# S4D convolution beside a gated linear unit on one core: 64-point sums of the spectra split by parity into 32-point sums

## The chip, the cores and the metric

One Trainium2 chip, one NeuronCore. The metric is the device time of one execution in microseconds (us), a median over runs; lower is better. Engines: PE (TensorE: matmuls; PEld is its weight load), DVE (VectorE), ACT (ScalarE), POOL (GpSimd), SP (SyncE, which issues most DMA transfers). Each engine takes its instructions in a fixed order and waits on semaphores. PSUM is PE's output memory, in banks of 2 KB a partition; SBUF is the working memory.

## What is computed

`u` is 2048 x 448 (L x D), N is 256, F is 1792. Cut to what matters:

```python
xn = layernorm(u)
dt = exp(log_dt); A = -exp(log_A_real) + 1j*A_imag; C = (C_real + 1j*C_imag)*dt[:, None]
P  = exp((A*dt[:, None])[:, :, None] * pos)               # D x N x L
K  = 2*einsum("dn,dnl->dl", C, P).real                    # the convolution's kernel
y  = irfft(rfft(xn.T, 2*L) * rfft(K, 2*L), 2*L)[:, :L].T  # causal convolution
out = u + y + xn*D_skip + (sigmoid(xn @ w_gate) * (xn @ w_up)) @ w_down
```

All matmul operands are 32-bit; the GLU's are split into a high and a low part (`xh`, `xl`, `wh`, `wl`, `dh`, `dl`, `hh`, `hl`), three products each.

## The kernel before

The Fourier transform of length 4096 is done as matrix products in stages. A first stage (of x in `x_spec` and `pair_first`, of K in `first_stage`) writes partial spectra to DRAM (`x1_d`, `sk_d`): for each of 33 residues k of the frequency a column of 64 blocks b, real and imaginary. The stage that the change is about, `spectra` (L850), then takes 17 steps. A step covers half of the channels (H = 224) and four residues k (one step holds the residue 32 of both halves). In a step:

- `loads` (L870) brings `sx` and `skl` (the partial spectra of x and of K) and the table `tb` of cosines and sines; loads stand three steps ahead (NLD = 3, L51).
- `there` (L896) does the 64-point sums over b: for each pair of residues and each of K and x it issues four matmuls of a 128x64 tile (L912; a matmul of 32-bit operands is two records in the trace, so 32 records a step), into PSUM tiles `sp` of one bank each, from a pool of four. ACT copies K's sum to SBUF (`kc`, L920). DVE forms the complex product of both: two products (L923, L924), reading x's sum in PSUM, a subtract and an add (L925, L926), into `yy`.
- `back` (L930) does the inverse sums of the product that the step before left in `yy`: eight matmuls of 64x128 tiles (L939), into tiles `pv` of the same four-bank pool. ACT copies them to `vt` (L948), and four transfers store them to `v_d` in DRAM (L959). `turned` (L961) loads `vp` from there in another order (L965).
- `last` (L967) does the last inverse stage once half of the channels is complete: 64 matmuls a half of 64x32 tiles (L976), added to the residual and GLU sums by DVE (L984).

In a step of the loop (L1006 to L1037) `back` of the step before comes first, then `there`, loads, at times `last`.

K itself comes from the kernel generator, `kgen` (L459): 56 chunks (NCK) of exponentials on ACT, DVE and POOL (L517, L526, L547, L550, L604 to L606) and matmuls `ko` (L620). After every four chunks `first_stage` issues 32 matmuls (64 records) of 64x64 tiles (`kp`, `kq`, L565), four tiles side by side.

The GLU is a second generator, `glu` (L733): `gate` (L699) issues 11 matmuls (L712) for the gate and 11 for the up product of 512 rows by 128 columns of F, then `th` on ACT (L720), `hf` on DVE (L723), `hh` on ACT (L728), `hl` on DVE (L730). The down matmuls `po` (L826) follow for a group of F tiles and are added to `acc` by DVE (L831). Some weights are split on the spot, not read back from DRAM: POOL loads them (`wraw`, L646 and L648), casts and subtracts (`wh` L774, `wl` L775), loads `rdw` (L654), casts and subtracts (`dh` L800, `dl` L801).

What sets the order: the main loop (L1138 to L1152) runs the two generators by pace. Each `yield` counts work units; the generator whose share of its `total` is smaller goes next. `total` of the convolution holds a term of 14 units ahead of the chunks, 56 x WK (5.5), and 17 x WS (4.5) for the spectra. `tc.issue_after` ties the matmuls of both to this order on PE; the order on DVE, ACT and POOL is fixed by a scheduler when the program is built. Buffers come from tile pools; a tile waits until all readers of the one that had its place before are done.

Of the kernel before, what the change touches and what calls it, by code (L numbers as in the profile page):

```python
# [15 lines left out]
ALU = mybir.AluOpType  # L16
# [14 lines left out]
WS = 4.5  # L31
HOLE = 6
WS = 4.5
# [24 lines left out]
def _tables():  # L58
# [16 lines left out]
    k2 = np.arange(64)[None, :]  # L75
    tab = np.zeros((NK1, 128, 128))
    bk = np.zeros((2, 2, 64, 2, 128))
    for q in range(NK1):
        al = 2 * np.pi * ((b * (q + 64 * k2)) % 4096) / 4096.0
        c, s = np.cos(al), np.sin(al)  # L80
        tab[q] = np.block([[c, -s], [s, c]])
        if q in (0, 32):


            for h in range(2):

                split = lambda t: t.reshape(64, 2, 32).transpose(0, 2, 1)
                both = lambda r, i: np.stack([split(r), split(i)], 3).reshape(64, 128)
                bk[q // 32, h, :, 0] = both(c.T, s.T)
                bk[q // 32, h, :, 1] = both(-s.T, c.T)  # L90

    tab[0, 64:] = 0.0
    t32 = np.concatenate([tab[32][:, None], bk[1].reshape(128, 2, 128)], 1)
    tab = tab[:32].reshape(8, 4, 128, 128).transpose(0, 2, 1, 3)

    wf = np.zeros((2, 2, 4, 8, 32, NA))
    for k in range(32):
# [5 lines left out]
        wf[:, 0, k % 4, k // 4] = re.reshape(2, 32, NA)  # L103
        wf[:, 1, k % 4, k // 4] = im.reshape(2, 32, NA)

# [7 lines left out]
    for row, tb_ in ((DC, 0), (64 + 2 * DC, 1)):  # L115
# [5 lines left out]
        "c_tab": f(tab, (8, 128, 4, 128)),  # L121
        "c_t32": f(t32, (128, 3, 128)),
        "c_bk": f(bk[0], (128, 2, 128)),
# [7 lines left out]
def s4d_glu_kernel(ctx, tc, io):  # L131
# [12 lines left out]
    x1_d = dram.tile([64, NB, D], F32, name="x1_d")  # L144
# [133 lines left out]
    def row(b, g):  # L278
        return 32 * (b // 4 % 2) + 8 * g + 4 * (b // 8) + b % 4
# [7 lines left out]
    def x_spec(xn, b0):  # L287

        for p in range(2):
# [7 lines left out]
            for i in range(2):  # L297
                r = row(b0 + i, 2 * p)
                nc.sync.dma_start(x1_d[:, r : r + 9 : 8], x1[64 * i : 64 * i + 64])
# [159 lines left out]
    def kgen(pk):  # L459
# [3 lines left out]
            ("sk", [128, 32, 32], F32), ("ks", [128, 8, 64], F32),  # L463
# [89 lines left out]
        def first_stage(bank):  # L553
# [7 lines left out]
            for s_ in range(8):  # L561
                for cc in range(2):
                    for r in range(2):
                        rows = slice(64 * r, 64 * r + 64)
                        nc.tensor.matmul(  # L565
                            pss[r][64 * cc : 64 * cc + 64, s_].rearrange("p j k -> p (j k)"),
                            ks[rows, s_], wk[rows, cc], start=True, stop=True,
                            skip_group_check=True,
                        )
# [13 lines left out]
        yield 14  # L583
        for g in range(NCK // NCH):
            for c in range(NCH):
# [42 lines left out]
                if cn % 4 == 3:  # L628
# [4 lines left out]
                    nc.scalar.copy(ks, ko)  # L633
# [53 lines left out]
    def pair_first(b, xns):  # L687
# [5 lines left out]
        for g in range(4):  # L693
            to = x1[:, g] if g < 2 else pg.tile([128, D], F32, name="x1", tag="rd", bufs=RB)
            nc.scalar.copy(to, pss[g][:, :D])
            for i in range(2):
                nc.scalar.dma_start(x1_d[:, row(b + i, g)], to[64 * i : 64 * i + 64])
# [35 lines left out]
    def glu():  # L733
        stores, later = [], []
        for half in range(2):
# [4 lines left out]
            for fs_ in ORDER[half]:  # L740
# [71 lines left out]
                for t in range(2):  # L812
                    acc = accs[2 * half + t]
                    for b in range(4):
# [21 lines left out]
                        if final and (t, b) == (1, 0):  # L836
                            sp_mm[:] = glu_mm
                            for m in range(0, 8, 2):
                                lasts[0](1, m)
# [10 lines left out]
    def spectra(pf):  # L850
# [4 lines left out]
        bk = const.tile([128, 2, 128], F32, name="bk", tag="wk", bufs=1)  # L855
        t32 = pg.tile([128, 3, 128], F32, name="t32", tag="rd", bufs=RB)
# [3 lines left out]
            "vt": [pf.tile([128, 2, 2, H], F32, name="vt", bufs=2)],  # L860
            "pd": [pf.tile([128, 2, H], F32, name="pd", bufs=2)],
            "yy": [pf.tile([128, 2, H], F32, name="yy", bufs=4)],
            "kc": [pf.tile([128, 2, H], F32, name="kc", bufs=3)],
        }

        def work(n, sh, bufs):
            return spare[n].pop() if spare[n] else pf.tile(sh, F32, name=n, bufs=bufs)


        def loads(h, k):  # L870
            sx = pf.tile([128, 4, H], F32, name="sx", bufs=NLD)
            sk = pf.tile([128, 7, 4, 32], F32, name="skl", bufs=NLD)
            if k == 32:

                nc.sync.dma_start(sx[:64, 0:2].rearrange("b h d -> b (h d)"), x1_d[32])
                for i in range(2):
                    nc.sync.dma_start(sk[:64, :, i], sk_d[64:, 7 * i : 7 * i + 7, 0])
                return t32, sk, sx
            ds, gs = slice(H * h, H * h + H), slice(7 * h, 7 * h + 7)
            nc.sync.dma_start(sx[0:64], x1_d[k : k + 4, :, ds].rearrange("k b d -> b k d"))  # L880
            nc.sync.dma_start(sx[64:128], x1_d[32 + k : 36 + k, :, ds].rearrange("k b d -> b k d"))
            if k not in tabs:
                tabs[k] = pf.tile([128, 4, 128], F32, name="tb", bufs=NTB)
# [6 lines left out]
        def bank(name):  # L890
            return psc[-1].tile([128, 2, H], F32, name=name, tag="sp", bufs=4)

# [3 lines left out]
        def there(k, tb, sk, sx):  # L896

            kk, np_ = (64, 64) if k == 32 else (128, 128)
            ys_ = []
            for j in range(2):  # L900

                ks = [(0, j, 0)] if k == 32 else [(2 * j + i, 2 * j + i, i) for i in range(2)]
                pss = []
                for src in (sk, sx):
                    ps = bank("sp")
                    with after():
                        for c in range(2):
                            for t, n, i in ks:
                                to, rhs = ps[64 * i : 64 * i + 64, c], sx[:kk, n]
                                if src is sk:  # L910
                                    to, rhs = to.rearrange("p (g d) -> p g d", d=32), sk[:kk, :, n]
# [268 lines left out]
```

## Time and profile before

| | us |
|---|---|
| median of three timed runs | 731.92 |
| lowest, highest of them | 731.25, 737.63 |
| profiled execution, first to last instruction (span) | 723.7 |
| median less span (start and end around the instructions) | 8.2 |
| stage 0 to 146: layer norm, preparation | 146.0 |
| stage 146 to 541: kernel generator | 395.0 |
| stage 541 to 546.2: gap | 5.2 |
| stage 546.2 to 700.3: spectra | 154.1 |
| stage 700.3 to 723.7: tail (last `vp`, `last`, output) | 23.4 |

The device time counts from the launch, the span from the first to the last instruction on the chip. The spectra are counted from the first `there` to the end of the last `back`; the generator from the first of its chunks. A line of a view of the trace names the source line, the engine, the tile that is written and those that are read, and behind "x" how many records it holds; what stands behind "<-" ended the idle time ahead of it. All shares are of the whole span unless a window is given.

### The profile page before, as it was taken

Reading aid. Unit: us, or ns where it says so; the run is one execution under the profiler, and the core shown is the slowest. Engines: PE = TensorE matmul, PEld = TensorE weight load, DVE = VectorE, ACT = ScalarE, POOL = GpSimd, SP = SyncE. Lnnn points to the kernel's source line nnn. Section 1 sums busy time; section 2 is a strip of 40 time slices with the busy share of each in tenths; the row PEclk is TensorE's granted clock in tenths of the full one; section 3 lists DMA queues with packets and bytes.
Section 4 is the critical chain, followed back from the end, with each engine's and each line's share of the span. In section 5 each row is a group of like instructions: output and inputs, shape, how many; then the busy total and the mean of one; then the engine's idle time right before and its main releaser. Section 6 shows DMA issues by size and latency. Waiting matters only on the chain.

```text
span 723.7 us, 19120 instructions
## 1 busy us (share of the span) xinstructions
PE 676.0 (93%) x7789; PEld 532.0 (74%) x7789; DVE 567.5 (78%) x778; ACT 420.8 (58%) x650; POOL 380.5 (53%) x425
## 2 busy tenths in 40 slices
PE   2898799997998999998999999999999999999996
PEld 1675688786876788565777887888877777767785
DVE  5799997699999999999589988987874555655544
ACT  3645455678677778899387777866742222322320
POOL 2120028699888778879646874785864000451002
PEclk9998899999999999999999999999999999999999
DMA  9946328534414445354753242232169999999745
GB/s 204 224 119 186 97 81 251 173 97 167 162 52 135 160 149 173 93 196 141 242 166 120 70 141 87 98 107 72 47 163 247 279 256 218 246 258 244 178 135 163
DMA packets 92711, 115.72 MB, mean 160 GB/s; under 512 B 12432, under 2 KB 81040, under 8 KB 92368
## 3 DMA queue, kind: packets, MB, share of 16 engines
q1 hardware_dynamic: 83040, 93.92, 47.4%
q10 hardware_dynamic: 7040, 14.91, 6.5%
q0 software_dynamic: 2544, 5.67, 3.2%
q8 instruction: 61, 1.00, 0.6%
q14 instruction: 26, 0.21, 0.1%
HBM read 69.70 MB, written 44.76 MB: 158 GB/s over the span
## 4 chain that ended last, share of the span: by engine, by line
PE 69%; DVE 13%; DMA 6%; ACT 5%; issue 3%; SPq 1%; POOL 1%; ACTq 0%; DVEq 0%; POOLq 0%
PE gu L712 28%; PE po L826 16%; PE sp L912 7%; PE ko L620 6%; PE pv L939 4%; PE tr L539 4%; DVE Ft L606 2%; DVE Et L604 2%; DVE Et L605 2%; DMA acc_d<-acc 1%; DVE hl L730 1%; DMA xe<-in_A_u_dram 1%; PE pv L976 1%; PE kp L565 1%; DVE m L321 1%
## 5 line engine op out<-in xcount | busy, mean ns | idle before, releaser
L517 POOL TENSOR_TENSOR me<-me,pm 128x32 f32<-128x32 f32 (+1 forms) x168 | 145.7, 867 | 85.0 <-DVE Et L605 72.9
L517 POOL TENSOR_TENSOR mf<-mf,pm 128x64 f32<-128x64 f32 (+1 forms) x112 | 120.7, 1078 | 4.9
L712 PE MATMUL gu<-xh,wh 128*128 128x512 f32 x336 | 100.3, 404 | 3.2 <-ACT xh L220 3.2
L712 PE MATMUL gu<-xh,wl 128*128 128x512 f32 x336 | 95.9, 393 | 0.0
L712 PE MATMUL gu<-xl,wh 128*128 128x512 f32 x336 | 95.1, 390 | 0.0
L826 PE MATMUL po<-dh,hh 128*128 128x448 f32 (+1 forms) x227 | 86.4, 380 | 6.1 <-DVE acc L831 2.5
L604 DVE TENSOR_TENSOR Et<-me,S 128x1024 f32<-128x1024 f32 x56 | 82.3, 1470 | 8.8 <-ACT S L550 4.5
L605 DVE TENSOR_TENSOR Et<-me,S 128x1024 f32<-128x1024 f32 x56 | 79.0, 1411 | 8.5 <-ACT me L530 7.6
L606 DVE TENSOR_TENSOR Ft<-mf,S 128x1024 f32<-128x1024 f32 x56 | 79.9, 1426 | 6.8 <-ACT S L550 4.4
L826 PE MATMUL po<-dl,hh 128*128 128x448 f32 (+1 forms) x227 | 84.2, 371 | 0.0
L826 PE MATMUL po<-dh,hl 128*128 128x448 f32 (+1 forms) x227 | 83.5, 369 | 0.0
L547 ACT ACTIVATE S<-tr 128x1024 f32<-128x1024 f32 x56 | 57.8, 1032 | 41.0 <-PE tr L539 33.4
L712 PEld LDWEIGHTS gu<-xh,wh 128*128 128x128 f32 x336 | 61.3, 190 | 22.3 <-ACT xh L220 4.6
L728 ACT CAST hh<-hf 128x512 fp32r<-128x512 f32 x56 | 35.0, 625 | 71.1 <-DVE hf L723 59.8
L712 PEld LDWEIGHTS gu<-xh,wl 128*128 128x128 f32 x336 | 63.3, 189 | 15.0 <-DVE pl L313 0.7
L620 PEld LDWEIGHTS ko<-Et,Ft 128*32 128x32 f32 x3584 | 53.5, 110 | 27.4 <-issue 17.1
L712 PEld LDWEIGHTS gu<-xl,wh 128*128 128x128 f32 x336 | 63.0, 188 | 14.0 <-issue 0.7
L620 PE MATMUL ko<-Et,Ft 128*32 128x64 f32 x3584 | 63.6, 222 | 9.2 <-DVE Ft L606 4.7
L723 DVE SCALAR_TENSOR_TENSOR hf<-th,gu 128x512 f32<-128x512 f32 x56 | 38.1, 680 | 37.4 <-PE gu L712 27.7
L550 ACT ACTIVATE S<-S,hpi 128x1024 f32<-128x1024 f32 x56 | 65.5, 1170 | 0.0
L831 DVE SCALAR_TENSOR_TENSOR acc<-po,acc 128x448 f32<-128x448 f32 (+1 forms) x81 | 48.7, 610 | 19.4 <-PE po L826 19.3
L730 DVE TENSOR_TENSOR hl<-hf,hh 128x512 fp32r<-128x512 f32 x56 | 51.2, 914 | 12.6 <-ACT hh L728 12.6
(199 smaller groups left out, 1288.6 us busy)
## 6 DMA issues: line engine op xcount, KB each, us to landing
sk_d<-sk ACTq DMA_DIRECT2D x14, 512.0 KB
sx<-x_d SPq DMA_DIRECT2D x32, 224.0 KB
skl<-sk_d SPq DMA_DIRECT2D x16, 448.0 KB
vp<-v_d SPq DMA_DIRECT2D x16, 448.0 KB
v_d<-vt SPq DMA_DIRECT2D x60, 112.0 KB
wt_d<-wh SPq DMA_DIRECT2D x9, 512.0 KB
wt_d<-wl SPq DMA_DIRECT2D x9, 512.0 KB
wl<-wt_d SPq DMA_DIRECT2D x9, 512.0 KB
```

The costliest lines, as they stand in the source:

```text
L517: ins = nc.gpsimd.tensor_tensor(m[:, :, w + a : 2 * w : n], m[:, :, a:w:n], par(base + i).unsqueeze(2).to_broadcast([128, 4 * DC, w // n]) ...
L547: nc.scalar.activation(rows(cs), pv, AF.Abs)
L550: sins[:] = [nc.scalar.activation(cs, cs, AF.Sin, scale=-TWO_PI, bias=hpi)]
L604: v.tensor_tensor(Et[:, :, :, 32:64], two(me[:, :, 32:64]), S[:, 1::-1], ALU.mult)
L605: v.tensor_tensor(Et[:, :, :, 0:32], two(me[:, :, 0:32]), S[:, 1:3, :, ::-1], ALU.mult)
L606: fts[:] = [v.tensor_tensor(Ft, two(mf), S[:, 3:5], ALU.mult)]
L620: nc.tensor.matmul(ko[32 * j : 32 * j + 32, sl], Ft[:, cc, DC * h + 4 * q + j], Et[:, cc, DC * h + 4 * q + j], start=(k == 0), stop=(k == ...
L712: glu_mm[:] = [nc.tensor.matmul(ps, a_, b_, start=(n == 0), stop=(n == len(mm) - 1))]
L730: v.tensor_tensor(hl, hf, hh, ALU.subtract)
L826: glu_mm[:] = [nc.tensor.matmul(po[:, ds], a_[:, bs], w_[:, ds], start=(n == 0), stop=(n == 3 * fc - 1))]
L831: v.scalar_tensor_tensor(acc[:, b, ds], po[:, ds], 0.5, acc[:, b, ds], ALU.mult, ALU.add)
L912: mm = nc.tensor.matmul(to, tb[:kk, t, 64 * c : 64 * c + 64], rhs, start=True, stop=True, skip_group_check=True,)
```

## The change

The 64-point sum over b is split by the parity of b: 32 even and 32 odd blocks lie in different partitions, each is summed over by a tile of its own, and the even and odd results are added for residue q + 64*k2, k2 below 32, and subtracted for k2 + 32. The tables halve accordingly (`c_tab` 8 x 128 x 4 x 64, 128 KB a load instead of 256).

- `there`: 32 matmuls (64 records) of 64x32 tiles instead of 16 of 128x64. Eight tiles lie side by side (two row groups, four column groups). All four banks are now one tile `pb` with one buffer. For K and for x: ACT copies the odd sums (`oo`, L909 of the new file), DVE adds and subtracts them and the even sums in PSUM (L911, L912). DVE forms the products (128 x 896, L916, L917), POOL the subtract and the add (L918, L919), and DVE again a sum and a difference for the inverse (`sd`, L921, L922).
- `back`: 16 matmuls (32 records) of 32x64 tiles (four row groups, two column groups) (L934), into the same `pb`; one ACT copy of 128 x 896 (L939), two transfers instead of four (L953).
- the loop: `back` stands in a block of its own, half of the step's units after `there`; `last` follows it. WS goes from 4.5 to 7.0, and the 14 units ahead of the chunks become 46 (AHEAD). In the order of PE, the kernel generator then has 660 gate and 336 down matmuls (719 and 384 before), the spectra 264 and 117 (198 and 81 before).
- `first_stage`: 64 matmuls (128 records) of 64x32 tiles, eight side by side, instead of 32 of 64x64; `ks` is copied by parity (L629).
- `x1_d` is laid out by parity: one store instead of two in `x_spec` and `pair_first`, and four `sx` loads of 32 partitions instead of two of 64.
- `last` takes its PSUM from `pb`; its output transfers go by four blocks instead of two.

Order of PE, a step in the middle of the spectra, before (`sp` is written by `there`, `pv` by `back`, `gu` by the gate matmuls):

```order
L939 MATMUL pv<-yy,bk 128x224 x8
L912 MATMUL sp<-skl,tb 64x224 x4
L912 MATMUL sp<-sx,tb 64x224 x4
L912 MATMUL sp<-skl,tb 64x224 x4
L912 MATMUL sp<-sx,tb 64x224 x4
L712 MATMUL gu<-xh,wh 128x512 x3
L712 MATMUL gu<-xr,wh 128x512
L712 MATMUL gu<-xh,wl 128x512 x3
L712 MATMUL gu<-xr,wl 128x512
L712 MATMUL gu<-xl,wh 128x512 x3
L939 MATMUL pv<-yy,bk 128x224 x8
```

The same place in the changed kernel (both write `pb`):

```order
L905 MATMUL pb<-skl,tb 32x224 x16
L905 MATMUL pb<-sx,tb 32x224 x16
L707 MATMUL gu<-xh,wh 128x512 x3
L707 MATMUL gu<-xr,wh 128x512
L707 MATMUL gu<-xh,wl 128x512 x3
L707 MATMUL gu<-xr,wl 128x512
L707 MATMUL gu<-xl,wh 128x512 x3
L934 MATMUL pb<-sd,bk 64x224 x16
```

`back` no longer stands right ahead of `there`: GLU matmuls (half a gate pair or more) lie between them on both sides.

Order of DVE in a step, before (`hf`, `hl` are the GLU's):

```order
L923 TENSOR_TENSOR yy<-kc,sp 128x448
L924 TENSOR_TENSOR pd<-kc,sp 128x448
L925 TENSOR_TENSOR yy<-yy 128x224
L926 TENSOR_TENSOR yy<-pd 128x224
L723 SCALAR_TENSOR_TENSOR hf<-th,gu 128x512
L730 TENSOR_TENSOR hl<-hf,hh 128x512
```

and in the changed kernel, with the start of the next step:

```order
L917 TENSOR_TENSOR kk<-kk,xx 128x896
L718 SCALAR_TENSOR_TENSOR hf<-th,gu 128x512
L921 TENSOR_TENSOR sd<-yy 128x448
L922 TENSOR_TENSOR sd<-yy 128x448
L725 TENSOR_TENSOR hl<-hf,hh 128x512
L911 TENSOR_TENSOR kk<-pb,oo 128x448
L912 TENSOR_TENSOR kk<-pb,oo 128x448
L911 TENSOR_TENSOR xx<-pb,oo 128x448
L912 TENSOR_TENSOR xx<-pb,oo 128x448
L916 TENSOR_TENSOR yy<-kk,xx 128x896
```

The two `sd` instructions, which read what POOL writes, stand ahead of the next step's reads of `pb`.

Order of POOL late in the program, before: only the GLU's weights.

```order
L774 CAST wh<-wraw 128x1024
L775 TENSOR_TENSOR wl<-wraw,wh 128x1024
L654 DMA rdw<-in_B_w_down_dram 128x448
L800 CAST dh<-rdw 128x448
L801 TENSOR_TENSOR dl<-rdw,dh 128x448
L646 DMA wraw<-in_B_w_gate_dram 128x3x128
L648 DMA wraw<-in_B_w_gate_dram 64x128 x2
```

In the changed kernel, from the subtract of step 3 to the one of step 4:

```order
L918 TENSOR_TENSOR yy<-yy 128x2x224
L769 CAST wh<-wraw 128x1024
L919 TENSOR_TENSOR yy<-kk 128x2x224
L770 TENSOR_TENSOR wl<-wraw,wh 128x1024
L650 DMA rdw<-in_B_w_down_dram 128x448
L795 CAST dh<-rdw 128x448
L796 TENSOR_TENSOR dl<-rdw,dh 128x448
L642 DMA wraw<-in_B_w_gate_dram 128x3x128
L644 DMA wraw<-in_B_w_gate_dram 64x128 x2
L642 DMA wraw<-in_B_w_up_dram 128x3x128
L644 DMA wraw<-in_B_w_up_dram 64x128 x2
L918 TENSOR_TENSOR yy<-yy 128x2x224
```

The weight work now stands between the spectra's subtracts and adds; like pieces stand at steps 4, 10 (also to 11) and 12.

The diff, cut to its core:

```diff
-WS = 4.5
+WS = 7.0
+AHEAD = 46
...
-            if k == 32:
...
-            nc.sync.dma_start(sx[0:64], x1_d[k : k + 4, :, ds].rearrange("k b d -> b k d"))
-            nc.sync.dma_start(sx[64:128], x1_d[32 + k : 36 + k, :, ds].rearrange("k b d -> b k d"))
+            for r, s in quarters:
+                nc.sync.dma_start(sx[s], x1_d[r + k : r + k + 4, :, ds].rearrange("k b d -> b k d"))
...
-                for cc in range(2):
+                for q in range(4):
                     for r in range(2):
                         rows = slice(64 * r, 64 * r + 64)
                         nc.tensor.matmul(
-                            pss[r][64 * cc : 64 * cc + 64, s_].rearrange("p j k -> p (j k)"),
-                            ks[rows, s_], wk[rows, cc], start=True, stop=True,
+                            pss[r][32 * q : 32 * q + 32, s_].rearrange("p j k -> p (j k)"),
+                            ks[rows, s_, q // 2], wk[rows, q % 2], start=True, stop=True,
...
+        pb = psc[-1].tile([128, 4, 512], F32, name="pb")
+        half = lambda t: t.rearrange("p (c d) -> p c d", c=2)
...
         def there(k, tb, sk, sx):
+            n = 2 if k == 32 else 4
+            np_ = 32 * n
+            both = []
+            for j, src in enumerate((sk, sx)):
+                with after():
+                    for c in range(2):
+                        for g in range(n):
+                            for p in range(2):
+                                s = slice(64 * p, 64 * p + 64)
+                                to = pb[32 * g : 32 * g + 32, 2 * j + p, H * c : H * c + H]
+                                rhs = sx[s, g]
                                 if src is sk:
+                                    to, rhs = to.rearrange("p (g d) -> p g d", d=32), sk[s, :, g]
+                                w = (t32[s, 0] if k == 32 else tb[s, g])[:, 32 * c : 32 * c + 32]
+                                mm = nc.tensor.matmul(to, w, rhs, start=True, stop=True, skip_group_check=True)
+                sp_mm[:] = [mm]
+                ev, od = (half(pb[:np_, 2 * j + p, : 2 * H]) for p in range(2))
+                oo = work("oo", [128, 2, H], 2)
+                nc.scalar.copy(oo[:np_], od)
+                t = work(("kk", "xx")[j], [128, 2, 2, H], 1)
+                v.tensor_tensor(t[:np_, 0], ev, oo[:np_], ALU.add)
+                v.tensor_tensor(t[:np_, 1], ev, oo[:np_], ALU.subtract)
+                both.append(t[:np_])
+            kk, xx = both
+            yy = work("yy", [128, 2, 2, H], 1)[:np_]
+            v.tensor_tensor(yy, kk, xx, ALU.mult)
+            v.tensor_tensor(kk, kk, xx[:, :, ::-1], ALU.mult)
+            nc.gpsimd.tensor_tensor(yy[:, :, 0], yy[:, :, 0], yy[:, :, 1], ALU.subtract)
+            nc.gpsimd.tensor_tensor(yy[:, :, 1], kk[:, :, 0], kk[:, :, 1], ALU.add)
+            sd = work("sd", [128, 2, 2, H], 2)
+            v.tensor_tensor(sd[:np_, 0], yy[:, 0], yy[:, 1], ALU.add)
+            v.tensor_tensor(sd[:np_, 1], yy[:, 0], yy[:, 1], ALU.subtract)
+            return sd
...
+        def back(h, k, sd, engs=(nc.sync, nc.sync)):
+            vt = work("vt", [128, 4, H], 2)
...
+                for e in range(2):
+                    for g in range(n):
+                        s = slice(32 * g, 32 * g + 32)
+                        for p in range(2):
                             mm = nc.tensor.matmul(
+                                pb[64 * p : 64 * p + 64, g, :H], bt[s, p, e], sd[s, p, e],
+                                start=(e == 0), stop=(e == 1), skip_group_check=True,
                             )
             sp_mm[:] = [mm]
+            nc.scalar.copy(vt[:, :n], pb[:, :n, :H])
...
             sp_mm[:] = glu_mm
-            if prev is not None:
-                back(*prev)
             cur = there(k, *ld[n])
...
+            glu_on[:] = [1]
+            yield WS / 2
+            sp_mm[:] = glu_mm
+            if prev is not None:
+                back(*prev)
...
-            glu_on[:] = [1]
-            yield WS
+            yield WS / 2
+            if due and n >= due[0]:
+                sp_mm[:] = glu_mm
+                for q in (0, 1, 2, 3)[2 * (n - due[0]) : 2 * (n - due[0]) + 2]:
+                    last(0, q)
```

More of the change, by code (lines that the diff above doesn't have):

```diff
@@ L30 @@
 WK = 5.5
-WS = 4.5
+WS = 7.0
 HOLE = 6
-WS = 4.5
+AHEAD = 46
 WP = 5
@@ L296, in x_spec @@
             nc.scalar.copy(x1, ps[:, :, :D])
[L297 to L299 removed]
+            r = row(b0, 2 * p)
+            nc.sync.dma_start(x1_d[:, r : r + 5 : 4], x1)
             yield WX
@@ L695, in pair_first @@
             nc.scalar.copy(to, pss[g][:, :D])
-            for i in range(2):
-                nc.scalar.dma_start(x1_d[:, row(b + i, g)], to[64 * i : 64 * i + 64])
+            nc.scalar.dma_start(x1_d[:, row(b, g)], to)
     def gate(w, xs, to, between=None):
```

191 lines of the change are left out of this document (74 added, 117 removed).

## The prediction

> **What bounds the kernel now.** I read the page's head first, then the busy times by stage (before the kernel generator, in it, the gap, the spectra, the tail), then the chain of waits in the spectra.
>
> ```profile
> span 723.7 us, 19120 instructions
> PE 676.0 (93%) x7789; PEld 532.0 (74%) x7789; DVE 567.5 (78%) x778; ACT 420.8 (58%) x650; POOL 380.5 (53%) x425
> ```
>
> In the next view the columns are window, its length, then busy time of PE, PEld, DVE, ACT and POOL, granted clock, DMA share and GB/s.
>
> ```profile
> 146.00:541.00 395.00, 379.23 (x5775) 302.83 (x5764) 350.07 (x359) 298.15 (x438) 300.36 (x317) 0.99 0.41 130
> 546.20:700.30 154.10, 153.35 (x1201) 116.05 (x1200) 88.59 (x173) 44.20 (x84) 30.31 (x36) 1.00 0.95 232
> ```
>
> PE is the bound by a wide margin in the spectra: 153.35 of 154.10 us, against 88.59 on DVE, 44.20 on ACT and 30.31 on POOL. Time taken from PE there is time gained until another engine or a wait takes over. In the kernel generator PE (379.23 of 395.00) is only 29 us ahead of DVE. The chain of waits gives the pieces of PE:
>
> ```profile
> 587.88 2.63 PE po L826 x13
> 590.50 1.71 PE pv L939 x16
> 592.22 3.18 PE sp L912 x32
> 629.90 5.21 PE gu L712 x22
> ```
>
> One step is a `there` (3.18), a `back` (1.71) and GLU work: a whole gate pair of 22 matmuls is 5.21, a down matmul 2.63/13 = 0.202. The median of the three timed runs is 731.92 us, 8.2 above the profiled span; I sum on the span and add 8.2.
>
> **The spectra's sums (the gain).** The new `there` has 64 records of 64x32 tiles, eight tiles side by side, the new `back` 32 records of 32x64 tiles, also eight. The kernel before already has such a form, in its last stage after the wait for its data (three windows of one burst, each from 708.85 us):
>
> ```profile
> 708.90 0.42 PE L976 MATMUL pv<-vp,wf 64*32 64x224 f32 x8 [0.91 <-DMA out_dram<-acc]
> 708.90 0.61 PE L976 MATMUL pv<-vp,wf 64*32 64x224 f32 x16 [0.91 <-DMA out_dram<-acc]
> 708.90 1.56 PE L976 MATMUL pv<-vp,wf 64*32 64x224 f32 x56 [0.91 <-DMA out_dram<-acc]
> ```
>
> Each further group of eight costs (1.56-0.42)/6 = 0.19 us. Eight groups are 1.52 us, 1.75 with the first one's latency; I take 1.70 for `there` and 0.92 for `back` (four groups, 0.76 to 0.99). The whole of that stage is the far end:
>
> ```profile
> 708.92 4.28 PE pv L976 x128
> ```
>
> That is 0.27 a group, so 2.14 and 1.07. Gain: 17 x (3.18-1.70) = 25.2 (bounds 17.7 to 28.2) and 17 x (1.71-0.92) = 13.4 (10.9 to 16.2). **-38.6 us on PE.** The last stage keeps its count of matmuls and its tiles: nothing.
>
> **First stage (kp, kq).** Its matmuls go from 32 to 64 in each of 14 groups, from four tiles to eight at once.
>
> ```profile
> 423.20 0.22 PE L565 MATMUL kp<-wk,ks 64*64 64x64 f32 x1
> 423.21 0.22 PE L565 MATMUL kq<-wk,ks 64*64 64x64 f32 x1
> 423.22 0.22 PE L565 MATMUL kp<-wk,ks 64*64 64x64 f32 x1
> 423.23 0.22 PE L565 MATMUL kq<-wk,ks 64*64 64x64 f32 x1
> 423.26 0.22 PE L565 MATMUL kp<-wk,ks 64*64 64x64 f32 x1
> ```
>
> Starts in different tiles lie about 0.01 apart and a turn of four takes 0.06 (423.20 to 423.26), so 64 records take 16 x 0.058 = 0.93. A turn of eight is the same 0.06 at best and 8 x 0.01 = 0.08 by the starts; I take 0.07: 16 x 0.07 = 1.12, **+2.7** over 14 groups (0 to +13, where eight records cost two turns of four).
>
> **The pace.** Later pacing moves GLU matmuls from the generator into the spectra (counted in the order: 59 gate and 48 down matmuls fewer in the generator, 66 and 36 more in the spectra, the rest in the gap). At 0.237 and 0.202 that is 23.7 us each way: nothing on PE. But the generator then holds 379.2-23.7+2.7 = 358 us of PE against some 339 on DVE (350.07 less five gate and five down evictions). PE idles 16 us there now; with the two so near it idles more: **+8** (0 to +16, twice the idle time). The first stage of x and the sx loads cut in four have slack: the loads are issued three steps ahead. **+1.4** for the tail (eviction by one copy of 896, then two transfers) and the start.
>
> **The step's new loop.** The even and odd sums must be combined from PSUM, multiplied, combined on POOL, then again on DVE, before `back` may start; and `there` and `back` share one set of four banks. So PE's `back` waits for the eviction of the `there` just ahead, and DVE runs that eviction only behind the sd instructions of the step before, which wait for POOL. Rows for it (line, shape, count, busy, mean ns), of the spectra:
>
> ```profile
> L923 DVE TENSOR_TENSOR yy<-kc,sp 128x448 f32<-128x448 f32 x32 | 19.7, 617 | 37.9 <-PE sp L912 37.9
> L925 DVE TENSOR_TENSOR yy<-yy 128x224 f32<-128x224 f32 x32 | 12.9, 404 | 0.0
> L730 DVE TENSOR_TENSOR hl<-hf,hh 128x512 fp32r<-128x512 f32 x10 | 8.5, 851 | 7.5 <-ACT hh L728 7.5
> L948 ACT COPY vt<-pv 128x448 f32<-128x448 f32 x31 | 15.0, 534 | 27.4 <-PE pv L939 27.4
> ```
>
> DVE's round: four evictions 4 x 0.62, two products of 896 at some 1.2 each (four times the row of 224, less its fixed part), POOL's add 1.13 (row below), two sd at 0.65, hl 0.85: 8.2 us. PE's round: 1.70+0.92+5.21 = 7.8. So DVE and POOL now set the pace by 0.4 a step, and vt, now one copy of 896 (0.9 to 1.07) queued behind hh, which waits for hf, holds the next `there` by as much: 0.8 over twelve steps, **+9.6** (0 to +20, the second if the products cost 1.5).
>
> Here a rule speaks against the change. The Trainium skill ("TensorEngine Tiling (Array Packing)", PSUM Bottleneck) says that packing tiles speeds up the matmuls but not the evacuation of PSUM, which may become the bottleneck. By that rule the ordinary steps cost the 9.6 above; without it (PE's round alone decides) they would cost nothing and the sum would be +0.9. The rows above side with the rule.
>
> **POOL's blocks (the largest loss).** POOL also prepares the streamed weights, in its own queue, and the two sd operations of a step now wait behind that:
>
> ```profile
> 644.60 1.04 POOL L774 CAST wh<-wraw 128x1024 fp32r<-128x1024 f32 x1 [5.04 <-PE pv L939]
> 645.72 2.37 POOL L775 TENSOR_TENSOR wl<-wraw,wh 128x1024 fp32r<-128x1024 f32 x1
> 648.38 0.58 POOL L654 DMA_DIRECT2D rdw<-in_B_w_down_dram  x1 [0.30 <-POOL wl L775]
> 653.87 0.55 POOL L800 CAST dh<-rdw 128x448 fp32r<-128x448 f32 x1 [4.91 <-DMA rdw<-in_B_w_down_dram]
> 654.51 1.13 POOL L801 TENSOR_TENSOR dl<-rdw,dh 128x448 fp32r<-128x448 f32 x1
> ```
> ```profile
> L648 POOL DMA_DIRECT2D wraw<-in_B_w_up_dram x6 | 3.1, 526 | 0.0
> L646 POOL DMA_DIRECT2D wraw<-in_B_w_up_dram x3 | 2.3, 779 | 0.0
> ```
> ```profile
> wraw<-in_B_w_up_dram POOLq DMA_DIRECT2D x6, 32.0 KB, 5.6
> ```
>
> An add or subtract on 128x448 is 1.13. Six issues are 2 x 0.78 + 4 x 0.53 = 3.7, the last lands about 5.6 after its issue. The places, in the order of POOL:
> - A, step 3 to step 4: subtract 1.13, wh 1.04, add 1.13, wl 2.37, issue 0.88, landing 4.91, dh 0.64, dl 1.13, six issues 3.7 = 16.9 from one subtract to the next. PE's work there, one `there`, one `back` and three gate halves, is 1.70+0.92+7.8 = 10.4: +6.5.
> - step 4 to 5: wh waits for the set just issued, then wl and the issue stand ahead of the next subtract: +1.
> - B, step 10: wh, between subtract and add, waits for weights issued just before: 5.6-1.13+1.04 = +5.5.
> - C, step 10 to 11: 2.37+0.88+4.91+0.64+1.13+3.7 = 13.6 against 7.8-1.1 = 6.7: +6.9.
> - D, step 12 to 13: 1.04+2.37+0.88+4.91+0.64+1.13 = 11.0 against 7.5 (a step with the last stage's matmuls in it): +3.5.
>
> **+23.4** (8, where half of a block overlaps banks already freed, to 32, where every landing takes 2 us more). What hid these blocks before was that no spectra work stood in POOL's queue.
>
> **The clock.** The granted clock falls when PE idles for some us:
>
> ```profile
> 78.00:85.00 7.00, 5.81 (x16) 5.20 (x17) 7.00 (x13) 0.34 (x1) 0.00 (x0) 0.51 0.56 150
> ```
>
> Seven us at 0.51 lose about 3.4. Two such spells in the spectra, after A and C, would be 7, shorter ones 2: I take **+4** (0 to +8).
>
> Sum: -38.6+2.7+8+1.4+9.6+23.4+4 = +10.5, span 734.2, with 8.2 outside 742.4; I say 742.
>
> **The rivals.** The stalls (the last three terms and the pace's 8) are 45 us; up to what size would the sign turn? The gain less the small terms is 38.6-2.7-1.4 = 34.5.
> - *Faster.* POOL's blocks are covered. The place is A to D: where the banks come free in time and rdw lands within the PE work, blocks are 5 us, without a spell of low clock, and the small stalls halve to 5. Then -34.5+8+5+5 = -16.5: 715.4 us. It decides from stalls (pace aside) of 19 us down. For it speaks the mean: POOL's 30.31 plus 17 x 2.26 = 69 of 150 us. Against it: each block lies within one step's chain, and no other queue does that work.
> - *The same.* The blocks cost half (12), the rest as summed: -34.5+8+9.6+12+2 = -3: 729.
> - *The change doesn't do what it says in `back`*: 32-row tiles in four row groups are seen nowhere in this trace, only 64-row tiles. If they go four at once, `back` stays at 1.71; PE's round is then 8.6 and outside the blocks it, not DVE, sets the pace: 12 x 0.4 + 1 = +6, 748 us.
> - *The first stage goes serially.* Each record waits for the one before at the spacing of the slowest spot in the rows (0.03 within the turn, 423.23 to 423.26): 128 x 0.03 = 3.8 against 0.93, 14 x 2.9 = +40, of which PE's slack to DVE hides a little: about 775. For it speaks nothing but the one gap; starts 0.01 apart speak against it. The Trainium skill ("TensorE: Matmul & The Clock Gate", Wait — 56ns, not 53.3ns?) gives a floor of about 25 ns from start to start for small matmuls; by an estimate from that page 128 records would take 3.2 us and the kernel some 30 us more. The trace disagrees for tiles side by side: its starts lie 10 ns apart.
>
> **How the numbers follow.** About 1% is what a measurement here can tell from no change: 724.6 to 739.2. Forecast, blocks of POOL and DVE's round eat the gain and more: 0.43. Faster 0.30. The same 0.17. `back` not packed 0.06, first stage serial 0.04. Slower by over 1%: 0.43+0.06+0.04 = 0.53. The sum of the terms' near ends runs from 712 (blocks and small stalls almost gone, generator free) to 758 (low clock and later landings, `back` as now); each side leaves out about 1 in 10. The forecast's own range is 738 to 752.
>
> **What would show it.** Right: `there` at 1.5 to 1.75 and `back` at 0.76 to 1.0 in the chain; PE's busy share in the spectra falls from 99% to below 85%; the waits show DVE's sd for POOL's yy with maxima of 5 us and over near steps 3, 10 and 12; POOL's dh waits 4.9 for rdw with a spectra subtract behind it; PE waits for DVE at `back` and for ACT's vt at `there`; the clock row shows dips within the spectra. Wrong: POOL waits gone from DVE's list, PE still 95% busy in the spectra and the span below 715 would mean that the banks or the loads were freer than I read; a `there` of 2.1 or more, or a kp group over 1.9, that PE's price was misread; a generator longer by over 16 us, that the pace costs more than the idle now shows.

## The result, and the profile after

The changed kernel takes **821.0 us** (median of four, 817.28 to 822.34) against 731.59 of the kernel before: a ratio of 1.124, with an interval of 1.117 to 1.131. The forecast was 742 (712 to 758). Its sign was right and its size, +10 for +89, was not.

The page's head of the profile after:

```profile
span 815.5 us, 22525 instructions
PE 686.1 (84%) x9477; PEld 523.1 (64%) x9477; DVE 607.4 (74%) x777; ACT 421.9 (52%) x635; POOL 427.3 (52%) x455
```

PE now idles in 16% of the span. The stages (columns as in the prediction's view): start, generator, gap, spectra, tail.

```profile
0.00:154.90 154.90, 124.88 (x559) 96.35 (x559) 126.26 (x231) 77.72 (x127) 46.67 (x69) 0.92 0.59 159
154.90:548.80 393.90, 365.18 (x6473) 288.84 (x6472) 331.43 (x343) 295.29 (x431) 279.60 (x294) 0.97 0.39 126
556.50:780.10 223.60, 167.10 (x2095) 115.61 (x2094) 138.92 (x186) 45.68 (x74) 95.02 (x84) 0.88 0.66 156
780.10:815.50 35.40, 21.95 (x206) 16.46 (x200) 9.25 (x17) 0.91 (x1) 3.30 (x6) 0.74 0.51 125
```

Between the first `ko` and the last, the generator of the kernel before takes 393.4 us (145.2 to 538.6). So: start +9.7, generator and gap +0.6 although 23.7 us of GLU matmuls were moved out of it, spectra +69.4, tail +12.1; together 91.8. The spectra lost the most: PE busy in 167 of 224 us, at a granted clock of 0.88 where it had been 1.00. PE's waits in spectra and tail, in the list of waits (total, times, longest):

```profile
PE pb L905 <- issue: 47.0, 17, 6.5
PE pb L970 <- DMA out_dram<-acc: 5.3, 1, 5.3
PE pb L970 <- DVE acc L979: 4.2, 2, 2.9
PE pb L970 <- DVE ac L979: 4.2, 3, 1.4
PE pb L934 <- DVE sd L921: 1.4, 1, 1.4
```

One wait makes up 47 of the 56.5 us, and it comes once in each of the 17 steps. "issue" says that the profile shows no releaser, so the timeline must. One step:

```profile
712.65 0.99 PE L905 MATMUL pb<-skl,tb 64*32 64x224 f32 x32 [1.34 <-DVE ac L979]
713.80 0.53 ACT L909 COPY oo<-pb 128x448 f32<-128x448 f32 x1 [5.99 <-PE pb L905]
714.36 0.62 DVE L911 TENSOR_TENSOR kk<-pb,oo 128x448 f32<-128x448 f32 x1 [1.77 <-ACT oo L909]
714.90 0.61 DVE L912 TENSOR_TENSOR kk<-pb,oo 128x448 f32<-128x448 f32 x1
715.62 1.87 PE L905 MATMUL pb<-sx,tb 64*32 64x224 f32 x32 [1.98 <-issue]
```

PE stops in the middle of `there`, between K's half and x's half. x's matmuls start 0.1 us after DVE has read the last of K's sums (714.90+0.61 = 715.51), though they write two other banks. The 2.0 us are what ACT's copy and DVE's two adds take, one behind the other. Both halves are parts of one tile, `pb`; in the kernel before each had a tile of its own. And x's half then takes 1.87 us, K's 0.99: the clock has fallen. The same after the first step's wait, on down matmuls:

```profile
563.66 0.57 PE L821 MATMUL po<-dh,hl 128*128 128x448 f32 x1
564.03 0.57 PE L821 MATMUL po<-dh,hh 128*128 128x448 f32 x1
...
565.42 0.36 PE L821 MATMUL po<-dh,hl 128*128 128x448 f32 x1
565.62 0.37 PE L821 MATMUL po<-dh,hh 128*128 128x448 f32 x1
```

Their starts lie 0.37 us apart, after 565 us 0.20. A wait of 3.0 us is followed by some 3 us at half speed.

Not every wait does this. The next two windows hold two and three of the 17 waits, each of 2.0 us and some 10 us from the next, and the granted clock stays at 1.00:

```profile
575.20:604.30 29.10, 25.08 (x312) 17.20 (x310) 20.27 (x25) 7.33 (x12) 18.32 (x16) 1.00 0.65 154
742.40:777.20 34.80, 28.78 (x398) 19.58 (x396) 21.23 (x32) 10.20 (x17) 11.07 (x8) 1.00 0.37 86
```

Of the 17 waits, the seven of 2.6 us and more are all followed by half speed. Of eight lone ones of 1.9 to 2.4 us, one is. The other two, of 2.0 us, stand close behind further gaps, and half speed follows: ahead of the one that ends at 715.62 us, shown above, lie three gaps of 1.1 to 1.4 us within 7 us. The Trainium skill ("TensorE: Matmul & The Clock Gate", HAM oscillation) has PE slow down at idle gaps of over some 3.4 us; here four waits of 2.6 to 3.3 us were enough, so the measurement goes further than that rule. Its next section (A second HAM failure mode: psum-queue depth-cycling) tells of frequent short idles with the same effect, which the place from 706 to 715 us bears out.

The tail shows the same tile at work in `last` (chain of waits, us and what):

```profile
796.10 1.90 PE pb L970 x32
...
798.56 0.62 DVE ac L979
799.18 0.04 issue
799.23 1.90 PE pb L970 x32
```

A quarter of `last` waits 1.3 us for the adds of the quarter ahead, at half clock; four quarters take 11.2 us (792.92 to 804.14) where 4.28 had done.

### The profile page after: what moved, and what is told of

It is laid out like the page before. It is cut to its first block, busy times and chain, and to the rows that moved or that the text cites. A ratio compares the mean times of both kernels' runs of the same rounds, so it can differ in the third digit from the quotient of the medians.

```text
span 815.5 us, 22525 instructions
## 1 busy us (share of the span) xinstructions
PE 686.1 (84%) x9477; PEld 523.1 (64%) x9477; DVE 607.4 (74%) x777; ACT 421.9 (52%) x635; POOL 427.3 (52%) x455
## 4 chain that ended last, share of the span: by engine, by line
PE 38%; issue 7%; DVE 6%; POOL 4%; ACT 3%; DMA 2%; SPq 0%; ACTq 0%; POOLq 0%; DVEq 0%
PE gu L707 15%; PE po L821 8%; PE pb L905 4%; PE ko L616 4%; PE tr L535 2%; PE pb L970 1%; ACT oo L909 1%; DVE Ft L602 1%; POOL me L513 1%; PE pb L934 1%; DMA v_d<-vt 1%; POOL yy L919 1%; DMA wraw<-in_B_w_up_dram 1%; POOL yy L918 1%; DVE yy L916 1%
## 5 line engine op out<-in xcount | busy, mean ns | idle before, releaser
L513 POOL TENSOR_TENSOR me<-me,pm 128x32 f32<-128x32 f32 (+1 forms) x168 | 148.2, 882 | 87.2 <-DVE Et L601 72.2
L707 PE MATMUL gu<-xh,wh 128*128 128x512 f32 x336 | 109.1, 435 | 7.4 <-DVE acc L826 4.8
L707 PE MATMUL gu<-xh,wl 128*128 128x512 f32 x336 | 100.8, 408 | 0.0
L707 PE MATMUL gu<-xl,wh 128*128 128x512 f32 x336 | 98.9, 399 | 0.0
L821 PE MATMUL po<-dh,hh 128*128 128x448 f32 (+1 forms) x227 | 89.9, 396 | 10.1 <-DVE hf L718 2.7
L602 DVE TENSOR_TENSOR Ft<-mf,S 128x1024 f32<-128x1024 f32 x56 | 82.8, 1478 | 13.9 <-issue 5.6
L601 DVE TENSOR_TENSOR Et<-me,S 128x1024 f32<-128x1024 f32 x56 | 79.3, 1415 | 14.2 <-ACT me L526 14.2
L918 POOL TENSOR_TENSOR yy<-yy 128x448 f32<-128x448 f32 (+1 forms) x17 | 32.3, 1898 | 106.7 <-DVE yy L916 106.6
L707 PEld LDWEIGHTS gu<-xh,wh 128*128 128x128 f32 x336 | 65.1, 205 | 31.9 <-issue 10.5
L600 DVE TENSOR_TENSOR Et<-me,S 128x1024 f32<-128x1024 f32 x56 | 76.4, 1367 | 8.4 <-ACT S L546 8.1
L707 PEld LDWEIGHTS gu<-xh,wl 128*128 128x128 f32 x336 | 67.1, 200 | 15.5
```

The lines of the kernel that those rows point to most:

```text
L513: ins = nc.gpsimd.tensor_tensor(m[:, :, w + a : 2 * w : n], m[:, :, a:w:n], par(base + i).unsqueeze(2).to_broadcast([128, 4 * DC, w // n]) ...
L600: v.tensor_tensor(Et[:, :, :, 32:64], two(me[:, :, 32:64]), S[:, 1::-1], ALU.mult)
L601: v.tensor_tensor(Et[:, :, :, 0:32], two(me[:, :, 0:32]), S[:, 1:3, :, ::-1], ALU.mult)
L602: fts[:] = [v.tensor_tensor(Ft, two(mf), S[:, 3:5], ALU.mult)]
L707: glu_mm[:] = [nc.tensor.matmul(ps, a_, b_, start=(n == 0), stop=(n == len(mm) - 1))]
L821: glu_mm[:] = [nc.tensor.matmul(po[:, ds], a_[:, bs], w_[:, ds], start=(n == 0), stop=(n == 3 * fc - 1))]
```

## Experiments

Each ratio is to the kernel before, run beside it on the same chip, with its interval. The kernel before took between 726.4 and 731.6 us there, so experiments that ran beside different ones are compared by ratio; 0.01 is some 7 us.

### e1 to e4: the tile, POOL, the pace

e1 cuts the tile in two:

```diff
-pb = psc[-1].tile([128, 4, 512], F32, name="pb")
+pb = [psc[-1].tile([128, 2, 512], F32, name=f"pb{i}") for i in range(2)]
...
-to = pb[32 * g : 32 * g + 32, 2 * j + p, H * c : H * c + H]
+to = pb[j][32 * g : 32 * g + 32, p, H * c : H * c + H]
...
-nc.scalar.copy(vt[:, :n], pb[:, :n, :H])
+for i in range(n // 2):
+    nc.scalar.copy(vt[:, 2 * i : 2 * i + 2], pb[i][:, :, :H])
```

> The changed kernel with the four-bank tile pb cut into two tiles of two banks, one for K's sums and one for x's; back's evictions become two copies of 128x448. Theory 1 (the second half of each there waits until the first half's sums have left PSUM, because both halves are one tile): the wait ahead of x's half, 2.0 us in each of 17 steps and 47 us in all, falls to below 15 us, PE's granted clock in the spectra rises from 0.88 to above 0.95, and the time falls from 821 to 745-765 us. Theory 2 (POOL's weight blocks are the loss): the wait only moves to back, and the time stays above 800 us. Theory 3 (the pace): above 790 us, with the spectra still starting after 555 us.

Measured: 763.3 us, 1.049 (1.040 to 1.057). Theory 1 holds. Spectra, tail and PE's waits in both:

```profile
554.00:734.60 180.60, 158.83 (x2095) 112.54 (x2094) 139.27 (x186) 46.81 (x89) 94.17 (x84) 0.94 0.80 195
734.60:761.60 27.00, 18.61 (x200) 15.64 (x200) 8.96 (x16) 0.97 (x2) 3.29 (x6) 0.88 0.59 155
```
```profile
PE pb L934 <- DVE kk L912: 9.5, 4, 4.6
PE pb L905 <- DVE ac L980: 4.3, 1, 4.3
PE pb L905 <- DVE acc L980: 2.7, 1, 2.7
PE pb L934 <- DVE sd L921: 2.6, 1, 2.6
```

The 17 waits are gone, the spectra are 43 us and the tail 8 us shorter, and the clock is at 0.94. (The expectation's 0.95 was missed by a little.) The banks written are the same four, so it is the shared tile, not a shared bank, that made x's half wait. By the ratios two tiles are worth 55 us. What is left is few and long.

e2 moves the subtract and the add of the complex product:

```diff
-nc.gpsimd.tensor_tensor(yy[:, :, 0], yy[:, :, 0], yy[:, :, 1], ALU.subtract)
+v.tensor_tensor(yy[:, :, 0], yy[:, :, 0], yy[:, :, 1], ALU.subtract)
```

and the add likewise.

> The changed kernel with the subtract and the add of the spectra on DVE instead of POOL. Theory 1: DVE's round gets 2.5 us longer and POOL's blocks no longer show; of the waits ahead of x's half only the part over 2.0 us goes, so the time moves by less than 15 us: 805 to 830 us. Theory 2: 775-795 us. Theory 3: as theory 1.

Measured: 808.2 us, 1.112 (1.104 to 1.120): within theory 1's figures. By the ratios it is 9 us below the changed kernel, but the two intervals overlap, and its spectra are only 5 us shorter (218.8 for 223.6). PE's list still begins with the wait between the halves:

```profile
PE pb L905 <- issue: 42.8, 17, 4.3
```

e3 and e4 change the pace alone, in the new and in the old kernel:

```diff
-WS = 7.0
+WS = 4.5
-AHEAD = 46
+AHEAD = 14
```

(e3; e4 has the reverse in the kernel before, with 46 for its two 14.)

> The changed kernel with the former pace: 4.5 units a step, 14 units ahead of the chunks. GLU work goes back from the spectra into the generator. Theory 3: the spectra start near 545-550 us as before, and the time falls by 20 us or more, to below 800 us. Theory 1: the waits of 2.0 us stay, with less GLU work beside them; within 10 us of 821. Theory 2: the same as theory 1, POOL's blocks between shorter steps cost slightly more.

> The kernel before with the new pace alone (7.0 units a step, 46 ahead of the chunks). Theory 3: slower than 731.6 by 15 us or more, since the generator no longer has GLU work to cover DVE. Theories 1 and 2: the pace costs 8 us or less (the forecast's term), so 730-742 us.

Measured: e3 838.3 us, 1.155 (1.150 to 1.161), slower than the changed kernel, so theory 3 falls as a cause of the whole; the theories that expected 821 within 10 were off too. Its spectra, with 23 us less GLU work, take 230.9 us at a clock of 0.80, not fewer than 223.6: GLU matmuls had filled time in which PE waited. e4: 741.3 us, 1.022 (1.016 to 1.027). That lies in the range of theories 1 and 2. But the kernel before took 726.4 beside it, so the pace costs 15 us, the least that theory 3 had; the forecast had 8. Its stages (start, generator, spectra):

```profile
0.00:155.10 155.10, 124.89 (x563) 96.39 (x564) 126.22 (x231) 77.73 (x127) 45.78 (x69) 0.92 0.60 159
155.10:532.60 377.50, 358.08 (x5641) 284.70 (x5640) 332.68 (x343) 294.17 (x430) 282.09 (x294) 0.97 0.43 132
540.00:715.90 175.90, 175.81 (x1303) 135.28 (x1302) 98.28 (x185) 47.22 (x89) 42.41 (x50) 1.00 0.85 209
```

The generator is 15.9 us shorter for 23.7 moved, so 7.8 are given back: the forecast's term. What the forecast lacked is the start, 155.1 for 145.2.

This gives the clean comparison for the spectra, same GLU work in both: 175.9 us with the old sums, PE busy throughout at clock 1.00, and 223.6 with the new ones, 56.5 of it idle.

### e5, e7, e8: what is left after the tile

e5 is e1 with e2's edit.

> The two tiles of e1, and the spectra's subtract and add on DVE instead of POOL. With the wait between the halves gone, e1 still has PE idle for 1.2 to 4.6 us at eight places in the spectra and the tail, 21 us in all, ahead of back or of the next there. Theory A (these are POOL's weight blocks): they fall to below 8 us and the time from 763 to 735-750 us. Theory B (DVE's round, 1.4 us longer with both operations in it, becomes the bound): 758-775 us, with many short waits instead of a few long ones.

Measured: 757.3 us, 1.035 (1.028 to 1.042), between the figures of the two theories. It is 6 us under e1 by the times and 10 by the ratios, with overlapping intervals: theory A's waits fell only in part (PE idle in the spectra 21.8 to 16.5 us). e7 and e8 go back to the old pace and to the old first stage, with its result stored in four pieces:

```diff
-ks[rows, s_, q // 2], wk[rows, q % 2], start=True, stop=True,
+ks[rows, s_].rearrange("p q b -> p (q b)"), wk[rows, cc], start=True, stop=True,
...
-nc.scalar.dma_start(sk_d[:, bank], tl["sk"])
+for cc in range(2):
+    for q in range(2):
+        nc.scalar.dma_start(
+            sk_d[64 * q + 32 * cc : 64 * q + 32 * cc + 32, bank],
+            tl["sk"][64 * cc + 32 * q : 64 * cc + 32 * q + 32],
+        )
```

> The two tiles of e1 with the former first stage (64x64 tiles, the result stored by four transfers in the order that the new spectra need) and the former pace. Theory A (first stage and pace add about 16 and 15 us to e1): 725-740 us. Theory B (neither adds by itself; what counts is the spectra): 750-765 us.

> e7 with the spectra's subtract and add on DVE. Theory A: as in e5 without POOL's blocks, 10 to 20 us below e7, 708-728 us, below the kernel before. Theory B (DVE's round is the bound with the shorter steps of the former pace): e7 or up to 15 us above it.

Measured: e7 771.5 us, 1.058 (1.053 to 1.062); e8 759.3, 1.039 (1.033 to 1.045). Both lie above every figure that I had for theory A, and e7 above theory B's too. e8 is under e7 by 12 us, as theory A had it: that is POOL's share at this pace. But with the old pace, the old first stage, two tiles and POOL out of the way, the new spectra still take longer than the old (e8):

```profile
564.00:732.60 168.60, 141.62 (x1992) 99.05 (x1992) 142.87 (x205) 43.57 (x83) 30.40 (x31) 0.86 0.83 202
```

168.6 us against 154.1, DVE busy for 143 of them. So the sum of parts that I had made for a good version was wrong, and the first stage had to be measured by itself.

### e6, e10 to e12: the first stage in the kernel before

e6 puts the 64x32 tiles into the kernel before; e10 keeps its 64x64 tiles and halves the columns, for as many matmuls; e11 and e12 put the first stage ahead in the order, with e6's tiles and with the old ones:

```diff
+for q in range(4):
...
+    pss[r][32 * q : 32 * q + 32, s_].rearrange("p j k -> p (j k)"),
+    ks[rows, s_, 32 * (q % 2) : 32 * (q % 2) + 32], wk[rows, q // 2], start=True, stop=True,
...
+for j in range(2):
+    pss[r][64 * cc : 64 * cc + 64, s_, j], ks[rows, s_], wk[rows, cc, 32 * j : 32 * j + 32],
...
-with hp(HP) if cn + 1 == NCK else tc.issue_after(glu_mm[0].ins):
+with hp(HP):
```

> The kernel before with only the first stage of K in 64x32 tiles, 64 matmuls a group instead of 32. Theory A (eight tiles run at once, a group takes 1.48 instead of 1.16 us): 14 x 0.32 = 4.5 us more at most, 728-734 us. Theory B (the generator of the changed kernel is 16 us longer than that of e4 at the same pace and the same GLU work, and the first stage is what differs: its bursts of 128 records push other work aside and outrun the fetching of PE's instructions): 10 to 27 us more, 738-753 us. Theory C (a floor of some 25 ns from start to start): 3.2 us a group, 29 us more, above 753 us.

> The kernel before with the first stage's 64x64 tiles kept, but each matmul cut in two of 32 columns: as many matmuls (64 a group) as in e6, the same results in the same places. Theory A (the number of matmuls is what costs, through PE's queue and the order of the other engines): within 8 us of e6, 747-763 us. Theory B (the narrow 64x32 tiles cost): at most 8 us over the kernel before, 725-738 us.

> e6 (64x32 tiles in the first stage of the kernel before) with the first stage put ahead of other ready work in the order, so that its matmuls stand in bursts close behind the chunk that feeds them. Theory A (the cost in e6 is one of order: DVE and ACT wait for GLU and phase matmuls that stand behind the spread-out first stage): below 745 us. Theory B (the matmuls cost by themselves, wherever they stand): 750 us or more.

> The control for e11: the kernel before with its own 32 matmuls a group put ahead in the same way. Theory A (order): differs from the kernel before by more than 5 us, either way. Theory B (the matmuls themselves): within 5 us of it.

Measured: e6 755.4 us, 1.036 (1.030 to 1.041); e10 763.9, 1.050 (1.047 to 1.053); e11 738.4, 1.016 (1.012 to 1.019); e12 742.4, 1.021 (1.017 to 1.024).

e6 costs 25 us where the forecast had 2.7. Its time is in theory C's range, its cost in B's (10 to 27). It is not the time of its matmuls, as C has it: a group of 128 records with nothing between takes 1.49 us (changed kernel), one of 64 takes 1.17 (before), so 14 x 0.32 = 4.5 at most:

```profile
550.00:551.49 1.49, 1.49 (x129) 1.00 0.05 11
```
```profile
539.89:541.06 1.17, 1.17 (x65) 1.00 0.00 0
```

128 records in 1.49 us are 11.6 ns each, so the rival of a serial first stage falls. The Trainium skill ("TensorE: Matmul & The Clock Gate", Wait — 56ns, not 53.3ns?) has about 25 ns from start to start as a floor; counted by records, eight tiles side by side lie at less than half of it here. A matmul is two records, so counted by matmuls it is 23 ns, close to that floor, and the forecast's estimate of 3.2 us from it had counted records. But the first records of eight different matmuls start within 0.05 us (549.98 to 550.03).

e10 shows that the cost doesn't need the narrow tile. But it isn't a clean test of the number of matmuls: it costs 10 us more than e6 by the ratios, just outside theory A, and a group of its records takes 2.13 us (574.96 to 577.09), so that some 13 of its 36 us are the matmuls themselves, an estimate over 14 groups. e11 has the same records as e6 and costs 15 us less by the ratios: where they stand counts. The control e12, the old first stage put ahead in the same way, costs 14 us for e11's 10, with overlapping intervals. The generators, before, e6 and e11:

```profile
145.20:538.60 393.40, 378.31 (x5746) 302.16 (x5749) 349.15 (x358) 297.38 (x437) 298.85 (x317) 0.99 0.41 130
```
```profile
148.60:570.30 421.70, 392.35 (x6582) 311.75 (x6581) 345.41 (x359) 298.97 (x438) 283.99 (x318) 0.96 0.39 122
```
```profile
147.40:546.90 399.50, 389.60 (x6582) 311.06 (x6581) 340.99 (x358) 299.19 (x438) 295.56 (x315) 0.98 0.41 128
```

e6's is 28 us longer: PE idles 14 us more and is busy 14 us more, at a clock of 0.96 for 0.99. DVE and ACT wait longer for PE than they did. In e6:

```profile
ACT sk L571 <- PE kq L565: 16.1, 7, 5.7
```
```profile
DVE hf L723 <- PE gu L712: 19.5, 10, 4.2
DVE acc L831 <- PE po L826: 13.2, 10, 3.7
```

and in the kernel before:

```profile
ACT sk L571 <- PE kq L565: 4.6, 2, 3.8
DVE hf L723 <- PE gu L712: 9.9, 7, 2.5
DVE acc L831 <- PE po L826: 3.9, 7, 1.4
```

ACT, DVE and POOL have fixed orders, and those changed with the matmuls as well: the scheduler placed them anew. That 15 of e6's 25 us go with the instructions' places is shown (e11); which of the moved ones does it, and what makes up the rest beyond the 4.5, is not. e6's theory B named the fetching of instructions too; no row here bears that out.

### e9, e13, e14: where PE's saving went

e9 is e5 with the former first stage. e13 leaves the subtract and the add out of it. e14 is e5 with e11's line.

> e5 (two tiles, combination on DVE, new pace) with the former first stage, stored by four transfers. Theory A (the new first stage costs the generator 10 to 16 us at this pace): the generator takes 372-382 us instead of 387, and the time falls from 757 to 738-750 us. Theory B (the four stores on ACT's queue take it back, as the generator of e7 and e8 suggests, 407 us against 393 before): 752-762 us.

> e9 without the subtract and the add of the complex product: this part of the computation is left out, so that DVE's round in a step loses two operations of 0.77 and 0.82 us and nothing else changes on PE, in the banks or in the transfers. Theory A (DVE's round sets the pace of the spectra, 152 of 178 us busy): the spectra fall from 170 us by 12 us or more, the time to 725-738 us, and PE's waits ahead of back go from 11 us to below 5. Theory B (the vt copies on ACT, the transfers at a share of 0.84 or the clock hold it): the time stays within 6 us of 749.7.

> e5 (two tiles, combination on DVE, new pace, new first stage of 128 records a group) with the first stage put ahead in the order as in e11. Theory A (order, not the matmuls): the generator falls from 387 us by 8 us or more and the time from 757 to 740-750 us, as e9 or below. Theory B: within 5 us of 757.

Measured: e9 749.7 us, 1.030 (1.027 to 1.034); e13 754.8, 1.039 (1.033 to 1.046); e14 762.5, 1.053 (1.046 to 1.060).

e9 at the new pace is the best version of the new sums, and at 1.030 it is no faster than the old sums at that pace (e4, 1.022; the intervals just touch). Between e5 and e9 the intervals overlap, and the spectra start only 2.4 us earlier (551.1 to 548.7), so although e9's time is in theory A's range, its generator didn't gain what A had: at this pace the first stage's price isn't resolved. e14 is above both its theories' figures and 13 us above e5 by the ratios, though the profiled executions are alike (754.0 and 753.4): "put it ahead" is no remedy in itself.

e13 refutes theory A, that DVE's round holds the spectra; its time is within theory B's 6 us. DVE falls from 150 to 127 us busy, and the spectra stay at 170.9 us (170.2 in e9). PE's waits and three pieces of e13's spectra:

```profile
PE pb L974 <- DMA vp<-v_d: 9.6, 1, 9.6
PE pb L937 <- DVE kk L917: 5.7, 1, 5.7
```
```profile
610.00:630.00 20.00, 20.00 (x314) 15.53 (x298) 17.30 (x28) 5.71 (x11) 0.00 (x0) 1.00 0.80 185
...
650.00:670.00 20.00, 9.87 (x176) 6.75 (x175) 6.56 (x10) 1.56 (x3) 6.43 (x10) 0.74 0.91 230
...
690.00:719.00 29.00, 29.00 (x426) 20.75 (x428) 23.84 (x37) 10.95 (x21) 0.00 (x0) 1.00 0.65 143
```

Where PE has no wait it is full at clock 1.00. Nearly all of the loss lies between 630 and 690 us. The largest piece is `last` of the first half, which waits for the load of `vp`: 9.6 us idle. In e9 that wait is 4.2 us. The chain of waits shows what it waits for: the last load of `vp` starts when a store of `v_d` has landed (650.24+6.69 = 656.93), and the matmuls follow it at 661.90.

```profile
650.24 6.69 DMA v_d<-vt
656.98 4.78 DMA vp<-v_d
```

So what DVE gave up came back as waits for transfers, with a lower clock behind them. What the best order of stores, loads and `last` would give wasn't tried.

## The forecast, step by step

- **The gain.** Right. With two tiles, a `there` without a wait runs from 705.50 to 707.24 in e1, 1.74 us for a forecast of 1.70; `back` is 1.01 (at 722.18 in the changed kernel) for 0.92.
- **The step's new loop** failed, and it is what made the forecast wrong. I wrote that "`there` and `back` share one set of four banks" and counted `there` as one block of eight groups. I never asked whether its second half may start while its first half is being read. It may not, as one tile: 47 us of waits, and with the clock and `last` 55 us in all by the ratios (e1). The kernel before couldn't show it in a row, but its code did: a tile a bank, "sp", four buffers, against one tile of four banks. In place of +9.6, this is 43 of the +69 in the spectra and 8 of the +12 in the tail. (22 of the +69 are GLU work moved in: 175.9 us in e4 for 154.1.) (22 of the +69 are GLU work moved in: 175.9 us in e4 for 154.1.) The sign that I had named, PE waiting for DVE at `back`, is 1.4 us in all in the changed kernel. My sum for DVE's round also left out `hf`, 0.68 us a step (38.1 us for 56 in the kernel before).
- **The clock.** +4 was far too low. At equal GLU work (e4 and the changed kernel) the new sums should have cut PE's 175.8 busy us by some 36, an estimate from 17 steps of 1.74 and 1.01 us in place of 3.18 and 1.71; they were 167.1. So some 28 us are lower clock. I had counted two long spells, behind blocks of 6.5 and 6.9 us; here every wait of 2.6 us and more is followed by one, and so are short waits close together.
- **POOL's blocks.** Right in kind, too large in size: +23 forecast; measured, 12 at the old pace (e7 to e8), and at the new one 9 (e2) and 10 (e1 to e5) by the ratios, both within overlapping intervals. DVE's waits for POOL's `yy` are there, 27.9 us with a longest of 4.9; that the wait between the halves and GLU work lay over much of them is argued, not shown.
- **The first stage.** +2.7 forecast. Its matmuls cost 4.5 at most (0.32 more a group, for 0.19 forecast). What the forecast had at nothing is the order of the instructions: e6 costs 25 us at the old pace, and e11 shows that 15 of them go with places.
- **The pace.** +8 for the generator is what e4 has (7.8). The start, +10, was missed: it's in the changed kernel (+9.7) as in e4.
- **The time outside the span.** The 8.2 us that the sum adds are not all start and end: each run has 1.8 us there (817.28 us for a span of 815.5). The rest is that the profiled execution of the kernel before was faster than its median.
- **The rivals.** `back` with 32-row tiles doesn't stay at 1.71 us: 1.01 is near the price of eight tiles at once. In the faster case POOL's blocks cost 5; they cost some 10, but the wait for the tile, which no rival had, outweighed that.

In ratios to the kernel before, the way back from the changed kernel is: 1.124, two tiles 1.049, POOL's part to DVE 1.035, the former first stage 1.030, and the pace with the old sums 1.022. The intervals of the second, third and fourth overlap from each to the next. No version here beats the kernel before.

## What to carry to other kernels

When buffers are merged for wider instructions, list for each write what now reads the same tile, not only the same bytes: a tile that is filled in two parts makes the second part wait for the readers of the first. Price a saving on the bound engine together with the waits that its shorter work uncovers, and count the clock behind each. More instructions in a program with fixed orders cost by where they push the others, so such an edit is measured by itself in the old kernel.

## What the runs showed of the chip

In the 17 steps PE ran at half speed behind every wait of 2.6 us and more: down matmuls 0.37 us apart, not 0.20. Lone waits of 1.9 to 2.4 us did so once in eight. Over the 224 us of the spectra the mean clock was 0.88. Eight tiles of 32 columns side by side took records at 11.6 ns each.
